# Converting the second layer's weights in three steps instead of two, and storing the experts' results one piece at a time

## The chip, the core and the metric

The kernel runs on one core of a Trainium2 chip. The time is device microseconds (us) from the start to the end of one execution. A core has five engines, each working through its own list of instructions in order: TensorE (PE; its weight loads are shown apart as PEld), VectorE (DVE), ScalarE (ACT), GpSimd (POOL), and SyncE (SP), which here does nothing but issue transfers. An instruction that waits holds up all that stand behind it on the same engine.

## The reference, cut to what matters

```python
attn = retention(q, k, v)               # state = gamma * state + k v^T ; y = scale * q state
x = attn as 1536 rows of 512
logits = x @ w_gate + softplus(x @ w_noise) * noise
top2, weights = the two best of 8 experts for each row, softmax over the two
for e in range(8):                      # D = 512, F = 1024
    h = max(x[mask] @ w1[e], 0)
    out[mask] += weight * (h @ w2[e])
h = out @ w_in                          # second layer: w_in 512x1024, w_out 1024x512
s = h * softmax(h);  ln = (s - mean) / sqrt(var + 1e-6) * g_ln
result = ln @ w_out
```

The two weights of the second layer, `w_in` and `w_out`, arrive as 64-bit floats, since the reference divides them by a square root in that type. The chip works on 32 bits, so the kernel converts them itself, with integer arithmetic.

## The kernel before

First comes the retention and the choice of experts (to about 98 us of the profiled execution), then eight experts one after the other (to about 376 us), then the second layer over twelve tiles of 128 rows.

**An expert** `e` is computed for up to `CAPS[e]` rows (448 falling to 384). Every 32-bit product is made of three matmuls: each operand is split into a high and a low part. The first half of an expert is eight blocks `hidden(e, f, ...)` (L709) of twelve matmuls each. A block ends in a PSUM bank; ACT writes the high part `hh` of the result (L722), then DVE the low part `hl` (L723). Even blocks use the two banks of tag `b`, odd blocks the two of tag `a`, so block f=4 can only start when `hl` of block f=0 is written. The second half is four calls of `second(e, j, py)` (L1051), 24 matmuls each, into four banks `c0` to `c3`.

**Weights.** An expert has eight units of 512 KB (units 8e to 8e+7). `load_unit` brings one into a tile `wr`, of which there are four; `split_unit` makes the high part `wh` on ACT (L194) and the low part `wl` on DVE (L195), and with that the `wr` is free for a later load. `advance(e, j)` (L1066) is called after every second block (j = 0 to 3) and after every `second` (j = 4 to 7): it splits units up to a bound out of the table `AHEAD` and issues loads to three units further. All loads of experts 2 to 7 are issued by SP.

**Rows.** The rows of expert e+2 are gathered by POOL while expert e is computed, stored to DRAM (`xs`, L999) and read back turned (`xq`, L1006), all by SP; `xg_t` (L1010) turns and splits the rows of the next expert behind the first and the second `second` of an expert: DVE L1023, ACT L1025, DVE L1026, four times.

**Results.** `y_t(e - 1, d)` (L1036) turns the result of the expert before into `yr` (DVE L1043, one buffer). It is called behind blocks 1, 3, 4 and 5 of expert e. The last call, behind block 5, issues four stores to `yg` from SP at once (L1047), ahead of the weight load of `advance(e, 2)`. `yg` is read back after the last expert.

**Conversion.** `convert_steps` (L93) is a generator over 16 jobs, 128 x 512 numbers each: eight of `w_in`, then eight of `w_out`. Each call of `convert()` runs it to the next `yield`. Before, a job has two steps. One step is three operations on DVE (L117, L118, L119) and one on ACT (L120), which needs the third. The other step is two operations on DVE (L123, L124), the first of which needs ACT's; then SP stores the result (L125) and loads the input of the job after the next (L102, two buffers). Six calls are made in expert 0, in `advance` of j = 4 to 7; then five in each expert, behind blocks 2 and 6 and in `advance` of j = 5, 6 and 7. Ahead of the last expert `for _ in conv` (L1129) runs what is left, which before is nothing. The second layer's weights are read back from DRAM by SP during the last expert (`w_in`, L174) and at its end (`w_out`, L176).

The order on each engine is the order of the calls in the program: nothing plans it anew.

Of the kernel before, what the change touches and what calls it, by code (L numbers as in the profile page):

```python
# [44 lines left out]
def retnet_moe_solu(ctx, tc, qT, kT, k, v, w_gate, w_noise, noise, w1, w2, w_in, w_out, g_ln,  # L45
                    decay, out, dbg=None):
    nc = tc.nc
    B, NC, _, H, D = v.shape
# [3 lines left out]
    E = w1.shape[0]  # L52
# [40 lines left out]
    def convert_steps():  # L93
        V = nc.vector
        cv = conv_ctx.enter_context(tc.tile_pool(name="cv", bufs=1, side="right", reuse_waits="tile"))
        view = lambda x, c: x.rearrange("(p r) f -> p (r f)", p=128)[:, c:c + 512]

        def load(n):
            if n < len(conv_jobs):
                w, _, c = conv_jobs[n]  # L100
                t = cv.tile([128, 512], I64, tag="raw", name="raw", bufs=2)
                nc.sync.dma_start(t, view(w, c))  # L102
                raws.append(t)

        raws = []
        load(0)
        for n, (w, f, c) in enumerate(conv_jobs):
            load(n + 1)
            yield
            raw = raws.pop(0)  # L110
            bits = raw.bitcast(I32).rearrange("p (n t) -> p n t", t=2)
            l, h = raw.bitcast(U32).rearrange("p (n t) -> p n t", t=2)[:, :, 0], bits[:, :, 1]
            m, e = (cv.tile([128, 512], I32, tag=t, name=t) for t in ("cm", "ce"))
            t = m.bitcast(F32)
            o = cv.tile([128, 512], F32, tag="co", name="co", bufs=2)

            V.tensor_scalar(m, h, 0xFFFFF, 1 << 20, op0=OP.bitwise_and, op1=OP.bitwise_or)  # L117
            V.scalar_tensor_tensor(t, l, 2.0 ** -32, m, op0=OP.mult, op1=OP.add)  # L118
            V.tensor_scalar(e, h, 0x7FF00000, None, op0=OP.bitwise_and)  # L119
            nc.scalar.activation(e, e, AF.Relu, bias=rebias, scale=8.0)  # L120
            yield

            V.scalar_tensor_tensor(e, h, -2 ** 31, e, op0=OP.bitwise_and, op1=OP.bitwise_or)  # L123
            V.scalar_tensor_tensor(o, t, 2.0 ** -20, e.bitcast(F32), op0=OP.mult, op1=OP.mult)  # L124
            nc.sync.dma_start(view(f, c), o)  # L125

    conv = convert_steps()

    def convert():
        next(conv, None)  # L130
# [74 lines left out]
    def feed(split_to, load_to, later=None):  # L205
        while feed_at[0] < min(split_to, n_units):
            while feed_at[1] <= feed_at[0]:
                load_unit(feed_at[1])
                feed_at[1] += 1
            split_unit(feed_at[0], later)  # L210
            feed_at[0] += 1
        while feed_at[1] < min(load_to, n_units):
            load_unit(feed_at[1])
            feed_at[1] += 1
# [367 lines left out]
    def add_table(lo, tag="a"):  # L582
        oh, nm = HOT.pop(lo)
        last = oh.shape[1] - 1
        p = bank(tag, (128, 32))
        for n in range(last + 1):
            nc.tensor.matmul(p, oh[:, n], nm[:, n], start=(n == 0), stop=(n == last))
        nc.vector.tensor_add(table, table, p)
# [3 lines left out]
    def by_rows():  # L592

        m = [128, 4, 32]
        nc.vector.tensor_mul(spread, part4[:, :, None].to_broadcast(m), table[:, None, :].to_broadcast(m))
# [113 lines left out]
    def hidden(e, f, c, between=None):  # L709

        xh, xl = xgT[e]
        hh, hl = H_t[e]
        early_part = not e and c.start == 0
        p = bank(("b", "c0", "b", "c1")[f % 4] if early_part else "ba"[f % 2])[:, :c.stop - c.start]

        terms = [(unit_t[8 * e + d][n], x, d) for x, ns in ((xh, (0, 1)), (xl, (0,))) for d in range(KD) for n in ns]
        for n, (w, x, d) in enumerate(terms):
            nc.tensor.matmul(p, w[:, 0, f * 128:(f + 1) * 128], x[:, d, c],  # L718
                             start=(n == 0), stop=(n == len(terms) - 1))
        if between:  # L720
            between()
        nc.scalar.activation(hh[:, f, c], p, AF.Relu)  # L722
        nc.vector.scalar_tensor_tensor(hl[:, f, c], p, 0.0, hh[:, f, c], op0=OP.max, op1=OP.subtract)  # L723
# [7 lines left out]
    def hidden_of(e):  # L731
        H_t[e] = (ep.tile([128, KF, CAP], F32R, tag="hh", name="hh"),
                  ep.tile([128, KF, CAP], F32R, tag="hl", name="hl"))
# [223 lines left out]
    xr_t, PY, yr_t = {}, {}, {}  # L957
# [78 lines left out]
    def y_t(e, d):  # L1036

        if d == 0:  # L1040
            yr_t[e] = ep.tile([128, CAP // 32, KD, 32], F32, tag="yr", name="yr")
        n = SETS[e]
        nc.vector.transpose(yr_t[e][:, :n, d], PY[e][d][:, :32 * n])  # L1043
        if d == KD - 1:
            dst = yg[OFF[e]:OFF[e + 1], :].rearrange("(b i) (a c) -> a i b c", i=32, a=4)
            for a in range(4):
                nc.sync.dma_start(dst[a], yr_t[e][32 * a:32 * a + 32, :n].rearrange("p b d j -> p b (d j)"))  # L1047
            yr_t.pop(e)
            PY.pop(e)

    def second(e, j, py):  # L1051

# [12 lines left out]

    def advance(e, j):  # L1066
        up = 8 * e + (AHEAD[j] if e or j > 3 else 5 + j)
        for n in range((0, 0, 0, 0, 2, 2, 1, 1)[j] if not e else j > 4):
            convert()
        feed(up, up + 3)  # L1070

    for e in range(E - 1):
        if e:
            hidden_of(e)
        for j in range(4):
            for f in (2 * j, 2 * j + 1):
                hidden(e, f, slice(0 if e else EARLY, CAPS[e]))
                if not e and f == 0:
                    todo = slots(10, NT)
                    next(todo)  # L1080
                if not e and f == 1:
                    next(todo, None)
                if not e and f == 3:
                    add_table(4, "c2")
                    add_table(10, "c3")
                    by_rows()
                if not e and f == 5:
                    lists()
                    for _ in load_xg(1):
                        pass  # L1090
                    rt_ctx.close()
                    gx["pool"] = gx_ctx.enter_context(tc.tile_pool(name="gx", bufs=1, side="right"))
                if e == 1 and f in (1, 3):
                    next(rows, None)
                if e and e + 2 < E and f < 4:
                    fresh = fresh if f else load_xg(e + 2)
                    nc.gpsimd.tensor_copy(pace, H_t[e][0][:1, f, :1])  # L1097
                    next(fresh)
                if e and f in (5, 7):
                    next(fresh, None)  # L1100
                if e and f in (1, 3, 4, 5):
                    d = (1, 3, 4, 5).index(f)
                    y_t(e - 1, d)
                    y_bank(e, d)
                elif e and f in (2, 6):
                    convert()
                elif not e and f > 5:
                    for d in ((0, 1), (2, 3))[f - 6]:
                        y_bank(e, d)
            advance(e, j)  # L1110
        for j in range(4):
            unit_t.pop(8 * e + j)
        xgT.pop(e)
        py = PY[e]
        for j in range(4):
            second(e, j, py)
            for d in ((0, 1), (2, 3), (), ())[j] if e else ((), (0, 1), (2, 3), ())[j]:
                xg_t(e + 1, d)
            advance(e, 4 + j)
            if not e:  # L1120
                fresh = fresh if j else load_xg(2)
                for n in range(2 if j < 2 else 1):
                    next(fresh)
                rows = fresh
            elif j in (1, 2):
                next(fresh, None)
# [4 lines left out]
    e = E - 1  # L1131
    hidden_of(e)
    for j in range(4):
        for f in (2 * j, 2 * j + 1):
            hidden(e, f, slice(0, CAPS[e]))
            if 0 < f <= KD:
                y_t(e - 1, f - 1)
            if f == 5:
                weights()
        advance(e, j)  # L1140
# [21 lines left out]
    for b in range(3):  # L1162
        py = bank(f"c{b}")
        c = slice(b * 128, (b + 1) * 128)
# [73 lines left out]
    with tc.If(full == 1), ExitStack() as fb_ctx:  # L1238
        fb = fb_ctx.enter_context(tc.tile_pool(name="fb", bufs=1))
        psum_pool(fb_ctx, "psum3", a=2, b=2, d0=1)  # L1240
        for g in range(NT // 4):
            xT = fb.tile([128, KD, 4, 128], F32, tag="fx", name="fx")
            acc, gate = [], []
            for n in range(4):
# [3 lines left out]
                p = bank("a")  # L1248
# [9 lines left out]
                a = fb.tile([128, DM], F32, tag=f"fa{n}", name="fa")  # L1258
# [10 lines left out]
            for e in range(E):  # L1269
                wa, wb = load_w(w1[e], w2[e])  # L1270
                h = fb.tile([128, KF, 512], F32, tag="fh", name="fh")
                for f in range(KF):
                    p = bank("b")
# [5 lines left out]
                for n in range(4):  # L1279
                    p = bank("a")  # L1280
# [6 lines left out]
            for n in range(4):  # L1287
                i = 4 * g + n
                x2T = fb.tile([128, DM], F32, tag="fr", name="fr")
                p = bank("a")  # L1290
# [12 lines left out]
                for f in range(KF):  # L1303
                    p = bank("a", (128, 128))
                    nc.tensor.transpose(p, z[:, f * 128:(f + 1) * 128], ident)
                    nc.vector.tensor_scalar_mul(zT[:, f], p, gcol[:, f:f + 1])
                p = bank("b")
                for f in range(KF):
                    nc.tensor.matmul(p, zT[:, f], wb[:, f], start=(f == 0), stop=(f == KF - 1))
                o = fb.tile([128, DM], F32, tag="fo", name="fo")  # L1310
# [57 lines left out]
```

## Time and profile before

| | us |
|---|---|
| three executions | 522.32, 525.71, 526.3 |
| their median | 525.71 |
| the profiled execution | 524.1 |
| its span in the trace | 522.5 |
| PE busy | 508.3 (97%) |
| DVE busy | 370.0 (71%) |
| ACT busy | 231.2 (44%) |

The span is the time between the first and the last instruction of the trace; 1.6 us of the execution lie outside it. The granted TensorE clock is 0.999 of full speed, so the engine's speed plays no part. A busy PE is not a PE at its peak: the ends of matmuls are modelled. Idle time of another engine costs something only where PE comes to wait for it.

### The profile page before, as it was taken

To read this page: it belongs to the slowest core of one execution; us is meant where nothing else is said; L and a number is where in the kernel's file an instruction comes from. 1 tells how busy PE (TensorE), PEld (TensorE's weight loads), DVE (VectorE), ACT (ScalarE), POOL (GpSimd) and SP (SyncE) were. 2 spreads that over 40 slices of the span, in tenths; PEclk is the share of its full clock that TensorE was granted. 3 is DMA by queue.
4 is the path that set the end of the run, shared out by engine and by line. 5 is a ranking of instruction groups with operands and counts; after the bars stand their busy time and mean duration, and the time that the engine had idled before them with its cause. 6 is when DMAs were issued, how large, how long until landed. Compare 5 with 4: busy or idle time off the path is not lost.

```text
span 522.5 us, 8643 instructions
## 1 busy us (share of the span) xinstructions
PE 508.3 (97%) x3068; PEld 462.9 (89%) x3068; DVE 370.0 (71%) x750; ACT 231.2 (44%) x435; POOL 102.5 (20%) x202
## 2 busy tenths in 40 slices
PE   9999999999999999999997999999999999999996
PEld 8888888999999999999997999998887788888886
DVE  5679888667668777877668778778367667766650
ACT  3487733435234335334244344354354535454441
POOL 4000001530302201204004000002244335511120
PEclk9999999999999999999999999999999999999999
DMA  8998431697897997969977987847462655563341
GB/s 252 336 398 311 167 112 52 191 346 236 263 316 178 334 319 164 336 218 221 375 241 204 325 222 213 243 143 194 150 207 58 204 166 143 169 188 102 100 122 46
DMA packets 71857, 111.92 MB, mean 214 GB/s; under 512 B 9760, under 2 KB 37152, under 8 KB 71808
## 3 DMA queue, kind: packets, MB, share of 16 engines
q1 hardware_dynamic: 65520, 94.58, 60.2%
q0 software_dynamic: 4944, 16.39, 9.8%
q8 instruction: 26, 0.43, 0.3%
q10 hardware_dynamic: 1344, 0.34, 0.3%
q14 instruction: 23, 0.19, 0.1%
HBM read 83.50 MB, written 27.79 MB: 213 GB/s over the span
## 4 chain that ended last, share of the span: by engine, by line
PE 41%; DVE 22%; DMA 17%; issue 8%; ACT 6%; SPq 4%; POOL 1%; POOLq 0%; DVEq 0%; ACTq 0%
PE b L946 12%; DMA wr<-in_moe_w_dram 9%; PE d L859 9%; DVE wl L195 4%; PE c L1060 3%; PE c L1174 3%; DVE xt L1023 3%; PE b L718 3%; DMA xq<-xs 2%; ACT wh L194 2%; PE a L718 2%; DMA xs<-xr 2%; PE s L426 2%; SPq L1047 2%; ACT xh L1025 2%
## 5 line engine op out<-in xcount | busy, mean ns | idle before, releaser
L195 DVE TENSOR_TENSOR wl<-wr,wh 128x1024 fp32r<-128x1024 f32 x68 | 81.8, 1219 | 30.6 <-ACT wh L194 26.3
L194 ACT ACTIVATE wh<-wr 128x1024 fp32r<-128x1024 f32 x68 | 70.1, 1051 | 33.6 <-DMA wr<-in_moe_w_dram 33.3
L1060 PE MATMUL c<-hh,wh 128*128 128x448 f32 (+5 forms) x224 | 79.2, 353 | 0.3 <-DVE c L1034 0.3
L1060 PE MATMUL c<-hl,wh 128*128 128x448 f32 (+5 forms) x224 | 78.8, 352 | 0.0
L1060 PE MATMUL c<-hh,wl 128*128 128x448 f32 (+5 forms) x224 | 78.7, 351 | 0.0
L718 PE MATMUL b<-xh,wh 128*128 128x192 f32 (+8 forms) x144 | 47.3, 337 | 3.6 <-DVE hl L723 3.2
L718 PE MATMUL b<-xh,wl 128*128 128x192 f32 (+8 forms) x144 | 46.8, 333 | 0.0
L1060 PEld LDWEIGHTS c<-hh,wh 128*128 128x128 f32 x224 | 42.0, 188 | 2.0 <-issue 0.6
L718 PE MATMUL a<-xh,wh 128*128 128x256 f32 (+7 forms) x128 | 43.1, 341 | 0.3 <-DVE hl L723 0.2
L1060 PEld LDWEIGHTS c<-hh,wl 128*128 128x128 f32 x224 | 42.1, 188 | 1.2
L1060 PEld LDWEIGHTS c<-hl,wh 128*128 128x128 f32 x224 | 42.1, 188 | 1.1
L718 PE MATMUL a<-xh,wl 128*128 128x256 f32 (+7 forms) x128 | 42.9, 340 | 0.0
L946 PE MATMUL b<-wh,zh 128*128 128x512 f32 (+1 forms) x104 | 38.5, 376 | 0.5 <-ACT zh L935 0.5
L859 PE MATMUL d<-wh,x2h 128*128 128x512 f32 x96 | 38.8, 404 | 0.0
L946 PE MATMUL b<-wl,zh 128*128 128x512 f32 (+1 forms) x104 | 38.4, 375 | 0.0
L859 PE MATMUL d<-wl,x2h 128*128 128x512 f32 x96 | 37.9, 395 | 0.0
L859 PE MATMUL d<-wh,x2l 128*128 128x512 f32 x96 | 37.8, 394 | 0.0
L1097 POOL COPY pace<-hh 1x1 f32<-1x1 f32 x20 | 8.7, 433 | 138.0 <-ACT hh L722 137.9
L120 ACT ACTIVATE ce<-ce,rebias 128x512 int32<-128x512 int32 x16 | 11.6, 723 | 54.1 <-DVE ce L119 51.3
L1025 ACT ACTIVATE xh<-xt 128x428 fp32r<-128x428 f32 (+5 forms) x24 | 13.0, 540 | 50.8 <-DVE xt L1023 50.8
L989 POOL DMA_INDIRECT xr<-xd,rows_r x27 | 30.1, 1116 | 14.8 <-issue 5.1
L872 ACT ACTIVATE ee<-d,st 128x1024 f32<-128x1024 f32 x12 | 13.4, 1118 | 41.8 <-DVE st L865 41.8
(259 smaller groups left out, 1096.3 us busy)
## 6 DMA issues: line engine op xcount, KB each, us to landing
wr<-in_moe_w_dram SPq DMA_DIRECT2D x60, 512.0 KB
zd<-zs SPq DMA_DIRECT2D x40, 128.0 KB
zc<-zd SPq DMA_DIRECT2D x10, 512.0 KB
xs<-xr SPq DMA_DIRECT2D x18, 256.0 KB
raw<-in_moe_w_in_dram SPq DMA_DIRECT2D x8, 512.0 KB
raw<-in_moe_w_out_dram SPq DMA_DIRECT2D x8, 512.0 KB
xq<-xs SPq DMA_DIRECT2D x16, 208.0 KB
yg<-yr SPq DMA_DIRECT2D x16, 208.0 KB
```

The costliest lines, as they stand in the source:

```text
L120: nc.scalar.activation(e, e, AF.Relu, bias=rebias, scale=8.0)
L194: nc.scalar.activation(hi, t, AF.Copy)
L195: low = lambda: nc.vector.tensor_sub(lo, t, hi)
L718: nc.tensor.matmul(p, w[:, 0, f * 128:(f + 1) * 128], x[:, d, c], start=(n == 0), stop=(n == len(terms) - 1))
L859: nc.tensor.matmul(PH[i][:, s, :], x[:, c], w[:, 0, f], start=(n == 0), stop=(n == 3 * KD - 1))
L872: nc.scalar.activation(ee, ph, AF.Exp, bias=col(0), accum_out=col(1))
L946: nc.tensor.matmul(p, z[:, f * 128:(f + 1) * 128], unit_t[8 * E + 4 + f // 2][n][:, f % 2, c], start=(m == 0), stop=(m == len(terms) - 1))
L989: nc.gpsimd.indirect_dma_start(out=t[b], out_offset=None, in_=xd[:], in_offset=bass.IndirectOffsetOnAxis(ap=rows_r[:, e - 1, b:b + 1], axi ...
L1023: nc.vector.transpose(t[:, :32 * n], xr_t[e][:, :n, d:128:KD])
L1025: nc.scalar.activation(hi, t, AF.Copy)
L1060: nc.tensor.matmul(py[d][:, :CAPS[e]], c, h[:, f, :CAPS[e]], start=(f == 0 and n == 0), stop=(f == KF - 1 and n == 2))
L1174: nc.tensor.matmul(py, h[:, f, c], w[:, f % 2], start=(f == 0 and n == 0), stop=(f == KF - 1 and n == 2))
```

## The change

Three things are changed.

A conversion job has three steps instead of two. The first step issues the store of the job before and does the three operations on DVE. The second issues the load for the next job and does ACT's operation. The third does the last two operations on DVE; their store is kept for the next job's first step. The first call of all only issues the first load.

The calls of `convert()` are spread otherwise: in expert 0 one for each `advance` of j = 4 to 7 (four), and in each expert from 1 to 6 seven: behind blocks 0, 2, 6 and 7, and in `advance` of j = 5, 6 and 7.

`y_t` becomes a generator. After the turn behind block 5 it stops; the four stores follow singly: behind `advance(e, 2)`, behind block 6, behind `advance(e, 3)`, and behind `advance(e, 4)`. For the result of expert 6, in the last expert, the four stores are issued at once as before.

```diff
         raws = []
         load(0)
+        store = None
         for n, (w, f, c) in enumerate(conv_jobs):
-            load(n + 1)
             yield
+            if store:
+                nc.sync.dma_start(*store)
             raw = raws.pop(0)
...
             V.tensor_scalar(e, h, 0x7FF00000, None, op0=OP.bitwise_and)
+            yield
+
+            load(n + 1)
             nc.scalar.activation(e, e, AF.Relu, bias=rebias, scale=8.0)
             yield
 
             V.scalar_tensor_tensor(e, h, -2 ** 31, e, op0=OP.bitwise_and, op1=OP.bitwise_or)
             V.scalar_tensor_tensor(o, t, 2.0 ** -20, e.bitcast(F32), op0=OP.mult, op1=OP.mult)
-            nc.sync.dma_start(view(f, c), o)
+            store = (view(f, c), o)
+        nc.sync.dma_start(*store)
...
+            y = yr_t.pop(e)
+            PY.pop(e)
             for a in range(4):
-                nc.sync.dma_start(dst[a], yr_t[e][32 * a:32 * a + 32, :n].rearrange("p b d j -> p b (d j)"))
-            yr_t.pop(e)
-            PY.pop(e)
+                if e < E - 2:
+                    yield
+                nc.sync.dma_start(dst[a], y[32 * a:32 * a + 32, :n].rearrange("p b d j -> p b (d j)"))
...
-        for n in range((0, 0, 0, 0, 2, 2, 1, 1)[j] if not e else j > 4):
+        if j > 4 or not e and j == 4:
             convert()
         feed(up, up + 3)
...
                     d = (1, 3, 4, 5).index(f)
-                    y_t(e - 1, d)
+                    y_st = y_t(e - 1, d)
+                    next(y_st, None)
                     y_bank(e, d)
-                elif e and f in (2, 6):
+                elif e:
                     convert()
+                    if f == 6:
+                        next(y_st, None)
...
             advance(e, j)
+            if e and j > 1:
+                next(y_st, None)
...
             advance(e, 4 + j)
+            if e and j == 0:
+                next(y_st, None)
```

## Rows read from the trace of the kernel before

**Rows 1.** The page: each engine's busy time, share of the span, instructions.
```profile
PE 508.3 (97%) x3068; PEld 462.9 (89%) x3068; DVE 370.0 (71%) x750; ACT 231.2 (44%) x435; POOL 102.5 (20%) x202
```

**Rows 2.** Waits of PE: who waited for whom, us, times, longest.
```profile
PE c L1060 <- DVE c L1034: 0.3, 1, 0.3
```

**Rows 3.** Timeline, PE, 205 to 323 us: start, length, instruction, idle before it.
```profile
206.57 0.45 PE L718 MATMUL b<-xh,wh 128*128 128x412 f32 x1 [0.56 <-DVE hl L723]
...
270.16 0.45 PE L718 MATMUL b<-xh,wh 128*128 128x396 f32 x1 [0.17 <-ACT xh L1025]
...
277.78 0.34 PE L718 MATMUL a<-xl,wh 128*128 128x396 f32 x1
280.74 0.45 PE L718 MATMUL b<-xh,wh 128*128 128x396 f32 x1 [2.62 <-DVE hl L723]
...
322.01 0.44 PE L718 MATMUL a<-xh,wh 128*128 128x388 f32 x1 [0.24 <-DVE hl L723]
```

**Rows 4.** Timeline, DVE, experts 4 to 5.
```profile
273.85 1.23 DVE L195 TENSOR_TENSOR wl<-wr,wh 128x1024 fp32r<-128x1024 f32 x1 [1.74 <-ACT wh L194]
274.99 0.68 DVE L123 SCALAR_TENSOR_TENSOR ce<-raw,ce 128x512 int32<-128x512 int32 x1
275.71 0.69 DVE L124 SCALAR_TENSOR_TENSOR co<-cm,ce 128x512 f32<-128x512 f32 x1
...
277.46 0.42 DVE L117 TENSOR_SCALAR cm<-raw 128x512 int32<-128x512 int32 x1
277.91 0.69 DVE L118 SCALAR_TENSOR_TENSOR cm<-raw,cm 128x512 f32<-128x512 uint32 x1
278.52 0.42 DVE L119 TENSOR_SCALAR ce<-raw 128x512 int32<-128x512 int32 x1
280.11 0.57 DVE L723 SCALAR_TENSOR_TENSOR hl<-b,hh 128x396 fp32r<-128x396 f32 x1 [1.18 <-ACT hh L722]
...
281.08 0.61 DVE L1043 STREAM_TRANSPOSE yr<-c 128x416 f32<-128x416 f32 x1
...
284.08 0.56 DVE L723 SCALAR_TENSOR_TENSOR hl<-b,hh 128x396 fp32r<-128x396 f32 x1
```

**Rows 5.** Timeline, ACT, the same stretch.
```profile
278.97 0.72 ACT L120 ACTIVATE ce<-ce,rebias 128x512 int32<-128x512 int32 x1 [4.20 <-DVE ce L119]
279.60 0.48 ACT L722 ACTIVATE hh<-b 128x396 fp32r<-128x396 f32 x1
```

**Rows 6.** Waits of ACT and of SP's queue, whole span.
```profile
ACT ce L120 <- DVE ce L119: 51.3, 15, 4.4
...
SPq L125 <- DVE co L124: 56.0, 13, 8.3
SPq L176 <- DVE wl L195: 37.4, 19, 8.9
```

**Rows 7.** Timeline, SP, expert 4: start, time of issue, instruction.
```profile
252.16 4.96 SPq L1047 DMA_DIRECT2D yg<-yr  x4
...
261.74 5.37 SPq L176 DMA_DIRECT2D wr<-in_moe_w_dram  x3
```

**Rows 8.** The chain that ended last, expert 4: start, us, what.
```profile
241.93 13.35 DMA wr<-in_moe_w_dram
```

**Rows 9.** Windows: length, then PE, PEld, DVE, ACT, POOL, clock, DMA share, GB/s.
```profile
249.00:256.00 7.00, 7.00 (x40) 7.00 (x39) 3.15 (x7) 1.22 (x3) 0.31 (x1) 1.00 1.03 401
...
270.00:277.00 7.00, 6.84 (x37) 6.84 (x38) 5.05 (x8) 2.73 (x4) 0.00 (x0) 1.00 0.33 75
```

**Rows 10.** Timelines of DVE and PE in the last expert.
```profile
344.58 0.56 DVE L723 SCALAR_TENSOR_TENSOR hl<-b,hh 128x384 fp32r<-128x384 f32 x1 [1.71 <-ACT hh L722]
346.60 0.56 DVE L723 SCALAR_TENSOR_TENSOR hl<-a,hh 128x384 fp32r<-128x384 f32 x1 [1.46 <-ACT hh L722]
...
354.92 0.56 DVE L723 SCALAR_TENSOR_TENSOR hl<-a,hh 128x384 fp32r<-128x384 f32 x1 [0.95 <-ACT hh L722]
...
360.74 0.33 PE L703 MATMUL a<-unit,causal 128*128 128x128 f32 x1
```

More of the change, by code (lines that the diff above doesn't have):

```diff
@@ L1136, in retnet_moe_solu @@
             if 0 < f <= KD:
-                y_t(e - 1, f - 1)
+                for _ in y_t(e - 1, f - 1):
+                    pass
             if f == 5:
```

## The prediction

> **What bounds the kernel now.** I read the page's busy times first: PE works 508.3 of 522.5 us [rows 1]. So PE sets the end, and a change that leaves its matmuls alone can only give back what PE stands idle in the stretch that the change touches. That is the second view, PE's waits, and its timeline over the experts. Five gaps are named there: 0.56, 0.17, 2.62 and 0.24 us, and 0.3 ahead of a first matmul into a result bank [rows 2, 3]. Together 3.9 us. After a gap the first matmul takes 0.45 instead of 0.34 us [rows 3], so each costs about 0.11 more. **About 4.4 us is all that the change can win among the experts**, although other engines wait far longer there: ACT 51.3 us for the third conversion operation, SP 56.0 us for the conversion's last [rows 6]. The reader should see these two sums and not take them for the prize: they are idle time of engines that are not the bound.
>
> Third, I asked the timelines of DVE and ACT what made the largest gap. In expert 5 block f=4 needs the low part of block f=0, which DVE writes at 280.11 [rows 4]. DVE was late because of three conversion steps between the experts: three operations (not shown again, the same as those at 277.46), two at 274.99, three at 277.46 [rows 4]. Twice DVE then stood idle, 1.74 us for the high part of a weight and 1.18 us for the high part of the block [rows 4], and both times that part stood on ACT behind the conversion's own operation, which had been waiting for DVE: 4.20 us before the second one, with the block's high part directly behind it [rows 5]. The two engines hold each other up in turn.
>
> **The change, part by part.**
>
> *Fewer conversion operations between two experts.* The first step is 0.42 + 0.69 + 0.42 = 1.53 us of DVE, the last 0.68 + 0.69 = 1.37 us [rows 4]. Between the `second` calls and block 0 of the next expert there were three steps out of two kinds, here 1.53 + 1.37 + 1.53 = 4.43 us. Afterwards the same three calls are, in whatever order, one of each of three kinds: 1.53 + 0 + 1.37 = 2.90 us. That is 1.53 us less.
>
> *ACT's operation a step later.* It now stands a call behind the DVE operation that it needs, and the two idle times of DVE, 1.74 + 1.18 = 2.92 us, have no cause left. In expert 5 it stands behind the high part of block 0, not ahead of it. Together with the step before, `hl` of block 0 comes 1.53 + 2.92 = 4.45 us earlier: it ends at 280.11 + 0.57 - 4.45 = 276.23 us. PE ran out of work at 280.74 - 2.62 = 278.12 us. The margin is 1.9 us, so the whole gap of 2.62 us goes. The gap at 206.57 has the same place between experts 2 and 3; the one at 322.01 comes in expert 6 behind an ACT operation of the conversion, which is no longer there at that block. I take out the three: 0.56 + 2.62 + 0.24 = 3.42, with 3 x 0.11 for the slow first matmuls **3.75 us**. The bounds are 0 (DVE late for other reasons) and 4.4 (all five).
>
> *Stores of the conversion and loads a step later.* SP no longer waits for work just given to DVE. The weight loads behind it, though, wait for `wl` as well, 37.4 us in all [rows 6], and `wl` comes out of the same list of DVE. PE waits for no weight at all. I take nothing; the bounds are 0 and the two gaps left, 0.17 + 0.3 with their slow matmuls 0.7 us. A load is issued two calls ahead of its use, as before, but calls are now seven and not five to an expert, so the notice falls by a third or so on average; at the shortest, from the last `advance` of an expert to block 2 of the next, lie three blocks. PE does 40 matmuls in 7 us [rows 9], so a block of 12 takes 2.1 us and the three 6.3 us. What covers a late load is the spare PSUM bank: about 2.1 us, worked out under the rivals.
>
> *Result stores singly.* The four took 4.96 us of SP's issue in expert 4 [rows 7], and the weight load of `advance(e, 2)` came behind them. It now comes about 5 us sooner. No wait of PE hangs on it, hence nothing. The load which was really late there, 13.35 us to land [rows 8], had been issued at 241.93, ahead of those stores.
>
> The DMA engines were fully busy around it, 1.03 by the share [rows 9], and what is moved ahead in the queue is only exchanged there for something else. The Trainium skill says as much ("DMA: Bandwidth & Descriptors", Issuing engines are not separate DMA queues): whatever engine issues them, transfers run on the same 16 DMA engines and interleave. By that rule the reordering of stores and loads gives no time; the row at 249 us agrees, the row at 270 us with its share of 0.33 shows that this does not hold for the whole stage.
>
> *What is left over for the last expert.* This speaks against the change. Sixteen jobs of three steps need 49 calls, counting the first load and the final store. There are 4 + 6 x 7 = 46. Three steps are therefore run at once ahead of expert 7: three operations on DVE, one on ACT, two on DVE, 1.53 + 0.72 + 1.37 = 3.62 us, which nothing separates [rows 4, 5]. And the last three calls of expert 6 now carry 2.90 us where before only one step of 1.37 us was left. That makes 3.62 + 2.90 - 1.37 = 5.15 us more in DVE's time ahead of 355 us. DVE's idle time there, waiting for blocks that PE had not finished, is 1.71 + 1.46 + 0.95 = 4.12 us [rows 10]. About 1.0 us is not covered and delays the small operations that build `causal`, which PE already takes up with hardly a pause at 360.74 [rows 10]. I put **+1.0 us** into the sum; bounds 0 (short idle times between DVE and ACT take it up) and 5.15 (none of the idle time serves). The blocks themselves have room: `hl` of block 0 would end at 344.58 - 1.71 + 5.15 + 0.56 = 348.6 [rows 10]; PE, done with block 0 at about 344, needs it three blocks later, at about 350.
>
> **The sum:** 524.1 - 3.75 + 1.0 = 521.35, which I give as **521.3 us** for the time of an execution. The sum starts from the profiled execution; the median of the three shown lies 1.6 us above it, at 525.71. I assume that the others differ by gaps of the same kind, so nothing is added. Against the median it is 4.4 us or 0.8% less. A difference under 1%, 5.26 us here, can't be told from no change; the limits are 520.45 and 530.97.
>
> **The rivals.**
>
> *More goes than the named gaps.* The window with a share of 0.33 shows DMA engines without work [rows 9]. If loads start earlier there, the two small gaps go too, and if DVE finds room before the last expert, the 1.0 us is not paid: 524.1 - 4.4 = 519.7. Against it: those loads waited for `wl`. Chance 0.14.
>
> *No change, since the DMA engines set DVE's pace.* DVE's lateness in expert 4 starts with the weight that took 13.35 us [rows 8]. If, with the engines full, it lands 2 us later still because other stores and loads stand ahead, the margin of 1.9 us is gone, and the 2.62 us gap stays or moves to another expert: between 524.1 and the median, 525.7. That is the rule cited above, taken as a mechanism. Chance 0.17.
>
> *Slower: the last quarter of the result is stored too late.* `yr` has one buffer. Its fourth store now stands behind the two loads of `advance(e, 4)`; in expert 4 three loads were issued from 261.74 to 267.11 [rows 7], so the store goes out at about 265.5. Block 1 of the next expert writes `yr` again, at 281.08 before [rows 4], some 4.45 us sooner afterwards: 276.6. That leaves 11.1 us for landing. `hl` of block 2 stands behind it, at 284.08 before [rows 4], hence ending at 284.08 + 0.56 - 4.45 = 280.2, and block 6 needs it two blocks after 278.12, at 282.3: 2.1 us of cover. From a landing time of 13.2 us on, each microsecond is lost at each of five such places. The longest landing above was 13.35 [rows 8]. At 16 us it would cost 5 x 2.8 = 14 us: 535. For it: a full DMA queue. Against it: one such landing was the exception. Chance 0.06.
>
> **How the numbers follow.** The forecast has 0.63; its own range is 519.7 (all five gaps, nothing paid in the last expert) to 523.4 (half of what lies between 1.0 and the bound of 5.15 paid as well, 2.1 us). About a third of it, 0.21, I place below 520.45, since the runs at 525.7 and 526.3 suggest that typical executions hold more waits than the profiled one. With the first rival that makes 0.35 for faster by over 1%. Slower by over 1% has 0.06. The rest, 0.59, is within 1%. The range reaches from 518.3, the first rival with a little for the spread of executions, to 525.6 at the no-change case.
>
> **What would show it.** Right: no gap of PE for `hl` between experts 4 and 5; ACT's wait for L119 far below 51.3 us; SP's wait for L124 nearly gone; conversion operations directly ahead of expert 7's first `hl`, and PE's transpose at L703 about 1 us later behind its matmuls. Wrong: a DVE wait at L1043 for a store, or at L117 for a load; new gaps of PE in the last expert; PE's gaps for `hl` as large as before.

## The result, and the profile after

| | before | after |
|---|---|---|
| median | 526.0 us (6 executions, 522.32 to 526.99) | 519.19 us (6 executions, 518.11 to 519.96) |
| profiled execution | 524.1 us | 519.29 us |
| its span | 522.5 us | 517.6 us |

The ratio is 0.989, with a 95% interval of 0.9859 to 0.992: about 1.1% faster. Timed once more beside the last experiments (e10), the changed kernel gave 0.9928 (0.9904 to 0.9952), so 0.7 to 1.1% is a fair size. The kernel before also varies more from execution to execution (519.4 to 527.0 over all that were run) than the changed one (518.1 to 520.3).

The page of the kernel after, engines' busy time; it answers to [rows 1]:

```profile
PE 506.3 (98%) x3068; PEld 462.9 (89%) x3068; DVE 370.1 (71%) x750; ACT 233.5 (45%) x435; POOL 98.4 (19%) x202
```

The number of instructions is the same on every engine; the span is 4.9 us shorter. To see where, one looks for PE's first matmul of each stage. Kernel before: second half of expert 0, expert 1, second layer.

```profile
98.80 0.37 PE L1060 MATMUL c<-hh,wh 128*128 128x448 f32 x1
...
120.10 0.36 PE L718 MATMUL b<-xh,wh 128*128 128x448 f32 x1
...
376.57 0.39 PE L859 MATMUL d<-wh,x2h 128*128 128x512 f32 x1
```

Kernel after, the same three places (line numbers are some 6 to 8 higher):

```profile
99.13 0.37 PE L1068 MATMUL c<-hh,wh 128*128 128x448 f32 x1
...
121.27 0.36 PE L724 MATMUL b<-xh,wh 128*128 128x448 f32 x1
...
371.75 0.39 PE L865 MATMUL d<-wh,x2h 128*128 128x512 f32 x1
```

The front end came 0.33 us later, the second half of expert 0 took 22.14 instead of 21.30 us (+0.84), experts 1 to 7 took 250.48 instead of 256.47 us (-5.99), and the second layer 145.85 instead of 145.93 us (-0.08). The sum is -4.90 us. All of the gain lies in experts 1 to 7: from first matmul to first matmul, experts 2, 3, 5 and 6 took 0.75, 0.83, 3.45 and 1.01 us less, and experts 1, 4 and 7 the same within 0.1 us.

PE's waits among the experts, kernel after; they answer to [rows 2, 3]:

```profile
PE a L1025 <- DVE xl L1032: 0.5, 1, 0.5
...
PE a L709 <- DVE causal L704: 0.2, 1, 0.2
```

None of the five gaps of before is left, not even the two that the prediction left in. There is one new gap in expert 0, of 0.55 us, which answers for most of the +0.84. (This stretch varies without any change to it: in the trace of e5, the same program up to there, it took 21.53 us.) Next DVE between experts 4 and 5; these rows answer to [rows 4]:

```profile
265.24 1.23 DVE L201 TENSOR_TENSOR wl<-wr,wh 128x1024 fp32r<-128x1024 f32 x1 [0.99 <-ACT wh L200]
266.39 0.68 DVE L128 SCALAR_TENSOR_TENSOR ce<-raw,ce 128x512 int32<-128x512 int32 x1
267.11 0.69 DVE L129 SCALAR_TENSOR_TENSOR co<-cm,ce 128x512 f32<-128x512 f32 x1
267.71 1.22 DVE L201 TENSOR_TENSOR wl<-wr,wh 128x1024 fp32r<-128x1024 f32 x1
268.85 0.42 DVE L119 TENSOR_SCALAR cm<-raw 128x512 int32<-128x512 int32 x1
269.31 0.69 DVE L120 SCALAR_TENSOR_TENSOR cm<-raw,cm 128x512 f32<-128x512 uint32 x1
269.91 0.42 DVE L121 TENSOR_SCALAR ce<-raw 128x512 int32<-128x512 int32 x1
271.32 0.57 DVE L729 SCALAR_TENSOR_TENSOR hl<-b,hh 128x396 fp32r<-128x396 f32 x1 [0.98 <-ACT hh L728]
```

DVE now stands idle ahead of `hl` because PE has only just finished the block, no longer because ACT is held up. ACT confirms it (answers to [rows 5]): its high part waits for PE, and the conversion's operation follows it.

```profile
270.78 0.50 ACT L728 ACTIVATE hh<-b 128x396 fp32r<-128x396 f32 x1 [4.62 <-PE b L724]
271.18 0.71 ACT L125 ACTIVATE ce<-ce,rebias 128x512 int32<-128x512 int32 x1
```

The 0.99 us ahead of the first `wl` are still ACT's: its conversion operation stood at 263.56, ahead of that weight's high part. The waits of ACT and SP after, against [rows 6]:

```profile
ACT ce L125 <- DVE ce L121: 11.7, 6, 4.1
ACT wh L200 <- DMA wr<-in_moe_w_dram: 8.7, 2, 7.6
...
SPq L182 <- DVE wl L201: 93.7, 26, 8.3
...
SPq L111 <- DVE co L129: 8.5, 5, 3.3
```

ACT's wait for the conversion fell from 51.3 to 11.7 us, SP's wait for its result from 56.0 to 8.5 us. SP waits more for `wl` instead, 93.7 against 37.4 us: it comes to its weight loads sooner and stands ready when a buffer is freed. And ACT's wait for weights from DRAM, not shown ahead of the prediction, is 8.7 us. Before it was:

```profile
ACT wh L194 <- DMA wr<-in_moe_w_dram: 33.3, 13, 5.8
```

Both waits left are in expert 0. From expert 1 on no weight is late. Two windows of the kernel after (columns as in [rows 9]) show DMA engines fully at work at 228 us and at 270 us, where the share in the second had been 0.33:

```profile
228.00:235.00 7.00, 7.00 (x40) 7.00 (x39) 5.60 (x8) 2.75 (x4) 0.00 (x0) 1.00 1.10 240
...
270.00:277.00 7.00, 7.00 (x41) 7.00 (x40) 4.43 (x8) 3.90 (x6) 3.52 (x5) 1.00 1.08 319
```

**One number for lateness.** How late DVE is can be read off the trace for each expert: from its first matmul to the end of its first `hl`. For expert 5 before, it is 280.11 + 0.57 - 268.75 = 11.93 us; after, 271.32 + 0.57 - 268.34 = 3.55 us. PE needs this `hl` after four blocks, that is after 9.3 us in expert 2, 8.6 us in expert 5 and 8.3 us in expert 7. One block, ACT's high part and DVE's low part alone make about 3.5 us, so 3.5 is the floor. For experts 2 to 7:

| kernel | 2 | 3 | 4 | 5 | 6 | 7 |
|---|---|---|---|---|---|---|
| before | 9.09 | 9.63 | 7.41 | 11.93 | 8.05 | 3.45 |
| after | 3.76 | 3.66 | 3.60 | 3.55 | 3.49 | 6.11 |
| e1_y_single | 8.91 | 8.53 | 7.18 | 9.59 | 8.02 | 3.44 |
| e2_conv_only | 3.78 | 3.66 | 3.60 | 3.54 | 3.49 | 6.12 |
| e3_act_early | 3.77 | 3.66 | 3.60 | 3.55 | 3.49 | 7.40 |
| e4_sp_early | 3.76 | 3.65 | 3.60 | 3.54 | 3.48 | 6.12 |
| e5_no_rest | 3.76 | 3.66 | 3.60 | 3.54 | 3.48 | 3.43 |
| e6_rest_two | 3.76 | 3.66 | 3.60 | 3.54 | 3.48 | 11.60 |
| e7_before_no_act | 5.29 | 4.66 | 3.60 | 3.54 | 3.49 | 3.43 |
| e8_before_sp_late | 5.52 | 4.67 | 4.02 | 5.60 | 5.17 | 3.43 |
| e9_spread_only | 3.76 | 3.66 | 3.60 | 3.54 | 3.49 | 7.40 |
| e10_changed | 3.76 | 3.66 | 3.61 | 3.55 | 3.49 | 6.12 |
| e11_before_sp_late | 6.57 | 5.71 | 4.36 | 5.61 | 5.16 | 3.42 |
| e12_convert_behind | 3.79 | 4.53 | 3.59 | 6.92 | 6.00 | 3.43 |

Each row is one traced execution. The traced execution of e1 is the fastest of its twelve (519.86 us), so its row is a mild case.

### The profile page after: what moved, and what is told of

Its sections match the earlier page's. It is cut to its first block, busy times and chain, and to the rows that moved or that the text cites. A ratio compares the mean times of both kernels' runs of the same rounds, so it can differ in the third digit from the quotient of the medians.

```text
span 517.6 us, 8642 instructions
## 1 busy us (share of the span) xinstructions
PE 506.3 (98%) x3068; PEld 462.9 (89%) x3068; DVE 370.1 (71%) x750; ACT 233.5 (45%) x435; POOL 98.4 (19%) x202
## 4 chain that ended last, share of the span: by engine, by line
PE 74%; DVE 13%; issue 6%; DMA 3%; ACT 2%; POOL 0%; SPq 0%; POOLq 0%; DVEq 0%; ACTq 0%
PE c L1068 18%; PE b L952 12%; PE b L724 11%; PE a L724 10%; PE d L865 10%; PE c L1190 3%; PE s L432 2%; DVE wl L201 2%; PE c L449 2%; DMA wr<-in_moe_w_dram 2%; PE c L460 1%; DVE pm L436 1%; PE c L445 1%; DVE rt L510 1%; PE c L482 1%
## 5 line engine op out<-in xcount | busy, mean ns | idle before, releaser
L728 ACT ACTIVATE hh<-b 128x192 fp32r<-128x192 f32 (+8 forms) x36 | 17.1, 476 | 43.6 <-PE b L724 40.6
L728 ACT ACTIVATE hh<-a 128x256 fp32r<-128x256 f32 (+7 forms) x32 | 15.9, 497 | 45.3 <-PE a L724 45.3
```

## The experiments

**Theory A**, the prediction's: DVE and ACT held each other up over the conversion, and there was too much of it between two experts. **Theory B**: SP's waits for the conversion held up weight loads, and late weights made DVE late.

| kernel | median, us | kernel before on the same chip, us | ratio, 95% interval |
|---|---|---|---|
| e1_y_single | 523.31 | 523.42 | 1.0004 (0.9976 to 1.0032) |
| e2_conv_only | 518.96 | 523.42 | 0.9907 (0.9872 to 0.9942) |
| e3_act_early | 520.14 | 523.42 | 0.994 (0.9915 to 0.9965) |
| e4_sp_early | 518.48 | 523.42 | 0.9907 (0.9874 to 0.9941) |
| e5_no_rest | 518.61 | 523.27 | 0.9926 (0.9899 to 0.9954) |
| e6_rest_two | 524.06 | 523.27 | 1.0011 (0.9987 to 1.0036) |
| e7_before_no_act | 518.51 | 523.27 | 0.9903 (0.9869 to 0.9937) |
| e8_before_sp_late | 518.06 | 523.27 | 0.99 (0.9867 to 0.9933) |
| e9_spread_only | 519.89 | 522.79 | 0.9955 (0.993 to 0.998) |
| e10_changed | 518.8 | 522.79 | 0.9928 (0.9904 to 0.9952) |
| e11_before_sp_late | 518.32 | 522.79 | 0.9921 (0.9893 to 0.995) |
| e12_convert_behind | 530.17 | 522.79 | 1.0147 (1.0106 to 1.0188) |

**Which part carries the gain: e1 and e2.** e1 puts only the changed `y_t` and its calls, as in the diff of the change, into the kernel before. e2 is the changed kernel with

```diff
-                if e < E - 2:
+                if e < E - 2 and a < 0:
                     yield
```

> The kernel before, with the experts' result stores singly as in the changed kernel and the conversion as it was. If DVE and ACT holding each other up over the conversion made the gaps (theory A), the gaps stay: 526.0 us, within 1 us, and ACT still waits about 50 us for the third conversion operation. If weight loads held up on SP made DVE late (theory B), the weight load that stood behind the four stores comes 5 us sooner and part of the gain is seen: 522 to 524.

> The changed kernel with the four result stores issued at once again. Theory A: all of the gain stays, 519.2 us, within 0.7. Theory B: 521 to 523, and gaps of PE for hl come back between experts.

e1 gave nothing beyond its interval of 0.3% either way, e2 all. The result stores, one half of the change's description, do not matter; it is the conversion.

**Inside the conversion: e3 and e4**, the changed kernel with ACT's operation early again, and with stores and loads early again:

```diff
 # e3
+            nc.scalar.activation(e, e, AF.Relu, bias=rebias, scale=8.0)
             yield
 
             load(n + 1)
-            nc.scalar.activation(e, e, AF.Relu, bias=rebias, scale=8.0)
             yield
 # e4
+            load(n + 1)
             yield
-            if store:
-                nc.sync.dma_start(*store)
...
-            load(n + 1)
...
-            store = (view(f, c), o)
-        nc.sync.dma_start(*store)
+            nc.sync.dma_start(view(f, c), o)
```

> The changed kernel with ACT's conversion operation back in the step of the three DVE operations; loads and stores stay a step later. Theory A: ACT's wait for DVE comes back, to about 50 us, and with it idle times of DVE of 1 to 2 us at each conversion; but between two experts only one such step is left instead of one or two, so part of the gaps comes back: 520 to 522.5. Theory B: no change from 519.2.

> The changed kernel with the conversion's stores and loads as before: the store right behind the last DVE operation, the next load right behind the store, ACT's operation still in a step of its own. Theory A: SP's wait for the last conversion operation comes back, some 40 us or more, and PE does not feel it: 519.2, within 0.7. Theory B: weight loads come late behind that wait: 521 to 524.

e4 agrees with theory A: SP waits 53.6 us for the conversion again, and the time does not feel it (518.48 us, at the lower edge of what was expected). e3 has the time that theory A gave, but not for its reason. ACT's wait is back, 46.1 us, and yet there is no gap between experts; the lateness is at its floor. What e3 loses (its median is 1.2 us above that of e2; the intervals overlap) is one wait in the last expert, for the small operations that build `causal` (1.48 us instead of 0.18); expert 7 takes 36.23 us in its trace and 34.91 in that of e2. So neither half is needed as long as the rest of the change, the new spread of the calls, stays.

**Each half alone in the kernel before: e7 and e8.** e7 takes out ACT's operation, e8 moves only stores and loads:

```diff
 # e7
-            nc.scalar.activation(e, e, AF.Relu, bias=rebias, scale=8.0)
 # e8
         load(0)
+        store = None
         for n, (w, f, c) in enumerate(conv_jobs):
-            load(n + 1)
             yield
+            if store:
+                nc.sync.dma_start(*store)
...
             nc.scalar.activation(e, e, AF.Relu, bias=rebias, scale=8.0)
+            load(n + 1)
             yield
...
-            nc.sync.dma_start(view(f, c), o)
+            store = (view(f, c), o)
+        nc.sync.dma_start(*store)
```

> The kernel before without ACT's conversion operation (the converted weights are then wrong; the DVE operations and all transfers stay). Theory A: ACT and DVE no longer hold each other up, hl of block 0 of expert 5 comes about 2.9 us sooner, and most of the gaps go: 520 to 522. Theory B: 525 to 526, since SP waits for DVE as before.

> The kernel before, two steps to a job and five calls to an expert, with only the stores and loads moved: the store in the next job's first step, the load behind ACT's operation of that step. Theory A: SP's wait for the last conversion operation falls from 56 us to under 15, and the time stays at 526, within 1. Theory B: 520 to 523.

Both give the full gain, 4.8 and 5.2 us. In this gain e7 was as theory A had it and e8 as theory B had it; their times lie below the ranges because the kernel before stood at 523.27 us this time, not at 526. e8 refutes theory A's claim that SP's part is worth nothing. e7 takes ACT's operation out; it does not move it a step later, as the change does, and that edit alone was not run. The timeline of DVE in e8, between experts 4 and 5, is the most telling of the study:

```profile
265.87 1.22 DVE L199 TENSOR_TENSOR wl<-wr,wh 128x1024 fp32r<-128x1024 f32 x1 [1.74 <-ACT wh L198]
...
272.14 0.57 DVE L727 SCALAR_TENSOR_TENSOR hl<-b,hh 128x396 fp32r<-128x396 f32 x1 [1.18 <-ACT hh L726]
```

The two idle times of [rows 4], 1.74 and 1.18 us, are there unchanged, to the hundredth, and so are the three conversion steps. But `hl` comes at 272.14 and not at 280.11, since everything ahead of it started earlier. So the three steps and the two idle times alone do not make a gap: DVE had come late to them. ACT's waits in e8 say why:

```profile
ACT ce L122 <- DVE ce L121: 49.9, 15, 4.4
ACT wh L198 <- DMA wr<-in_moe_w_dram: 6.1, 4, 3.4
```

The weights are no longer late: 6.1 us of waiting against 33.3. Note that e7, which touched no transfer, also lowered that wait, to 19.6 us. That led to **theory C**, a ring: late weights make DVE late, a late DVE frees the weight buffers late, so SP issues the next loads late, and weights come late. ACT's operation in its old place and SP's wait are two links.

The traces show the links. A unit's load needs the `wr` of the unit four before, so it can't go out ahead of the end of that unit's `wl`. One turn of the ring in the kernel before, three loads into the same buffer (the first went out at 241.93 [rows 8], the second at 261.74 [rows 7]); ACT, DVE, DVE, SP, ACT:

```profile
255.30 1.06 ACT L194 ACTIVATE wh<-wr 128x1024 fp32r<-128x1024 f32 x1 [5.78 <-DMA wr<-in_moe_w_dram]
...
256.39 1.23 DVE L195 TENSOR_TENSOR wl<-wr,wh 128x1024 fp32r<-128x1024 f32 x1 [4.11 <-ACT wh L194]
...
276.32 1.22 DVE L195 TENSOR_TENSOR wl<-wr,wh 128x1024 fp32r<-128x1024 f32 x1
...
279.87 3.54 SPq L176 DMA_DIRECT2D wr<-in_moe_w_dram  x2
...
288.84 1.06 ACT L194 ACTIVATE wh<-wr 128x1024 fp32r<-128x1024 f32 x1 [2.45 <-DMA wr<-in_moe_w_dram]
```

The late weight holds up DVE for 4.11 us and frees its buffer at 257.62; the load at 261.74 is split behind the conversion steps by 277.54; the next goes out at 279.87 and is late again. Over the loads of units 16 to 59, counted in the traces from the first matmul of the expert before, the loads of e8 go out 5.7 us earlier on average than in the kernel before. Of this, 1.7 us are SP's shorter delay once the buffer is free (1.99 instead of 3.68 us), and 4.0 us are buffers freed earlier. In e7 SP's delay is nearly what it was (3.45 us), and the loads still go out 4.4 us earlier.

**The third cut: e9, and controls.** e9 makes both edits, ACT's of e3 and SP's of e4; e10 is the changed kernel itself, e11 is e8 again.

> The changed kernel with neither of the two cures: ACT's conversion operation stands in the step of the three DVE operations, and store and load go out as before, the store right behind the last DVE operation. What is left of the change is that seven calls instead of five share the work, and the result stores singly. Theory C, formed after the first eight runs: late weights make DVE late, a late DVE frees the weight buffers late, and so weights come late; ACT's operation in its old place and SP's wait are two links of that ring, and either cut ends it. If the ring needs both links and they are back, the gaps are back: 522 to 524. If the even spread is a third cut (one conversion job between two experts instead of one and a half, 1.5 us less of DVE), 519 to 521.

> The changed kernel itself, for comparison on the same chip: 519.2, within 1.

> The kernel before with only the conversion's stores and loads a step later, once more, beside the changed kernel: 518.1, within 0.7, so about 1 us below the changed kernel, which has the leftover ahead of the last expert and a late weight in expert 0.

e9 keeps ACT's wait (46.1 us) and SP's (47.7 us), and the lateness is at the floor in experts 2 to 6. Seven short steps instead of five, and one conversion job between two experts instead of one and a half, are enough alone (the result stores singly, which e9 keeps too, gave nothing in e1). Which of the two it is, the fewer operations between experts or the even spread, was not separated. So two of the change's parts suffice each alone (e8, e9), and so does taking out what the third one moves (e7). The median of e9 is still 1.1 us above that of e10 (the intervals overlap, but 11 of e9's 12 executions lie above 519.5 us and 10 of e10's 12 do not), for a reason that is not between experts; its longest wait of PE:

```profile
PE a L705 <- DVE causal L700: 1.5, 1, 1.5
```

It is the same wait as in e3, and the lateness of expert 7 is the same, 7.40 us. Both kernels have the leftover ahead of the last expert together with ACT's operation in its old place; a run of them without the leftover was not made. e11 and e10 can't be told apart: the gain of about 1 us that I expected for e11 was 0.5 us, within the intervals.

**The leftover: e5 and e6**, with three calls more and three less.

```diff
 # e5, e6
                     y_bank(e, d)
+                    if e > 3 and f == 4:     # e5
+                        convert()
                 elif e:
-                    convert()
+                    if e < 6 or f == 7:      # e6
+                        convert()
```

> The changed kernel with three more calls of the conversion, one behind block 4 of experts 4, 5 and 6, so that nothing is left ahead of the last expert. If the leftover costs 1.0 us, as the sum of the prediction had it, 518.2; if DVE's spare time covers it, 519.2, within 0.5. The three operations and ACT's should be gone from the place ahead of the last expert.

> The changed kernel with three calls less in expert 6 (none behind blocks 0, 2 and 6), so that two whole jobs are left ahead of the last expert instead of one. hl of its block 0 ended 2.2 us ahead of PE's need; the second job adds 3.6 to 4.4 us there, so if each job costs DVE and ACT its full length, PE waits 1.4 to 2.2 us for hl: 520.6 to 521.4. If the spare time there is larger than I count: 519.2.

In e5 the leftover is gone (lateness 3.43 in expert 7). Its median lies between the two times expected and can't decide; the traces do: expert 7 takes 34.86 us in e5 and 34.93 in the changed kernel, so one job left over costs less than 0.1 us there. Two jobs cost 5.45 us against e5, more than double of what I expected. Why, DVE's row ahead of the last expert in e6 and PE's gap show:

```profile
344.76 0.43 DVE L119 TENSOR_SCALAR cm<-raw 128x512 int32<-128x512 int32 x1 [1.79 <-DMA raw<-in_moe_w_out_dram]
```

```profile
348.99 0.69 PE L724 MATMUL b<-xh,wh 128*128 128x384 f32 x1 [3.17 <-DVE hl L729]
```

The second job's input is loaded inside the leftover, so DVE had to wait 1.79 us for it, which I had not counted. The rest is the clock, below. This trace is of the slowest execution of e6 (525.99 us), and expert 7 takes 41.14 us in it, 6.28 more than in e5.

**Another order: e12.**

```diff
-        for n in range((0, 0, 0, 0, 2, 2, 1, 1)[j] if not e else j > 4):
-            convert()
         feed(up, up + 3)
+        for n in range((0, 0, 0, 0, 2, 2, 1, 1)[j] if not e else j > 4):
+            convert()
```

> The kernel before with one thing changed: in advance, the conversion's call stands behind the weights' splits and loads, not ahead of them. SP's loads no longer queue behind the conversion's store there, and DVE frees the weight buffers first; the step's contents stay, and so does ACT's wait. Theory C: that cuts the ring at the same link as the later store: 518 to 520. If the later store worked by something else: 523 to 526.

It is slower by 1.5%, through one gap in expert 0 that neither side had foreseen:

```profile
DVE cm L117 <- DMA raw<-in_moe_w_in_dram: 5.8, 1, 5.8
```

```profile
123.35 1.97 PE L1019 MATMUL a<-unit,xr 128*128 128x128 f32 x8 [8.80 <-DVE xl L1026]
```

The conversion's first loads now stood behind three weight loads, went out at 113.37, and DVE waited for them with the split of expert 1's rows behind it. After that there is no gap between experts, but a pause of 8.8 us gives DVE time to catch up in any case, which no run tells apart from a cut of the ring. So for theory C this run is inconclusive. It does show the price of a conversion load that comes late, a risk that the prediction covered with "about 2.1 us".

## Why the prediction was right, step by step

The time lies in the range, 2.1 us below the forecast. It lies below 519.7 too, where the forecast's own range ended: only the first rival, with its chance of 0.14, reached down to it. The change was 1.1% faster; I had put 0.59 on less than 1% and 0.35 on more. So the direction and the stage were foreseen, but that the time fell into the range is in part luck: the ring, of which a single cut gives the whole gain, is not in the prediction.

- **PE bounds, and only its gaps can be won.** Right. Its gaps among experts 1 to 7 are gone, and that is the gain. The bound of 4.4 us was too low: experts 1 to 7 gained 5.99 us. Measured from start to start against the usual distance, PE lost 5.7 us from expert 1 to expert 6 before and nothing after. A named gap cost about 0.27 us on top of its length (2.88 for that of 2.62), not 0.11, and two delays in expert 2, together 0.58 us, were too short to be named.
- **Fewer operations between experts.** Right, and worth more than its 1.53 us: in e9, where it comes with the even spread alone, the lateness is at the floor.
- **ACT's operation a step later.** Right in sign as far as known: without the operation (e7) the loss is gone; the move alone was not run. The working was wrong: the two idle times of DVE, 1.74 and 1.18 us, were not what made the gap, since e8 has both and no gap, and afterwards 0.99 and 0.98 us of them were still there. `hl` of expert 5 came 8.4 us earlier against PE (11.93 to 3.55), where the step gave 4.45 with the one before. The rest is the weights that are no longer late.
- **Stores and loads of the conversion a step later: nothing.** This step was wrong as I put it. Taken alone it gives the whole gain (e8). It adds nothing only where the other two are there (e4). I had argued that loads wait for `wl` as well, which comes from DVE; that is true, but it closes a ring, and I read it as a reason that nothing could be won. That DVE's lateness in expert 4 starts with the late load of 241.93 stands in the prediction only as a rival's reason for no change; why that load was late I did not ask.
- **Result stores: nothing.** Right (e1, e2).
- **The leftover ahead of the last expert: +1.0 us.** Mis-sized. The lateness of expert 7 rose by 2.66 us (3.45 to 6.11), and PE's wait for `causal` was 0.18 us. Without the leftover expert 7 takes 0.07 us less (e5). The estimate comes nearer where ACT's operation stands in its old place: there the wait is 1.48 and 1.49 us (e3, e9).
- **Expert 0** was not in the sum: it cost 0.84 us in this trace.
- **The signs.** Those for right came, but for the transpose at L703, which waited 0.18 us and not 1. Two of those for wrong came, both too small to matter: one DVE wait of 0.2 us for a conversion load, and PE's 0.18 us in the last expert.
- **The clock** was read off one trace (0.999) and left out of the sum. In many executions of the kernel before it was lower; see the last section.

So the sum was -3.75 + 1.0 = -2.75 us. Measured between the profiled executions: -4.81 us.

Of the rivals, *more goes than the named gaps* came nearest: the two small gaps went, the leftover was not paid, and the DMA engines worked where they had idled. It gave 519.7; the profiled execution took 519.29. *The DMA engines set the pace* did not happen: weights came on time with the same bytes. The Trainium skill's rule there ("DMA: Bandwidth & Descriptors", Issuing engines are not separate DMA queues) says on which engines transfers run, not what a load loses while it waits to be issued; they idled part of the time, with a share of 0.33 in one window [rows 9]. That a new order of stores and loads gives no time, as the prediction concluded from it, does not hold here: e8 changes only the order in which they are issued and gains 5.2 us. *The last quarter stored too late* did not happen: no wait of DVE at the turn into `yr` appears.

What stays open: whether the ring is the whole cause of the late weights, and how much each link adds. Each of three cuts brings the lateness under PE's need in every expert, though not to the floor in e7 and e8, and the traces show the links and loads that go out earlier; no run changes the number of `wr` buffers, which would be another cut. Open, too, is why experts 1 and 2 take 0.77 and 0.51 us longer in the traces of e2, e7 and e12 than in all others that have no gap there; no wait is named.

## What to carry to other kernels

When two engines and a load queue wait for each other in a circle, lateness can be handed on from stage to stage, and one small cut can end it, as each of three did here; three cures are then not worth three times one. Before costing a queue's wait at nothing because another wait stands beside it, follow who that other one waits for, and see whether the chain comes back. And measure the slack by one number per stage, such as the time from the first matmul to the first result written: it shows how near to the edge a kernel stands (6.11 of about 8.3 us in the last expert here) where the time does not.

## What the runs showed of the hardware that was not expected

A pause of PE can cost more than its length. In e6 (columns as in [rows 9]) the windows around the 3.17 us gap are:

```profile
336.00:345.00 9.00, 9.00 (x54) 9.00 (x53) 5.67 (x10) 1.38 (x2) 0.00 (x0) 1.00 0.58 179
345.00:349.00 4.00, 0.83 (x6) 0.51 (x4) 3.14 (x7) 2.71 (x5) 0.00 (x0) 0.91 0.00 1
349.00:355.00 6.00, 6.00 (x19) 6.00 (x20) 6.00 (x9) 2.86 (x5) 0.00 (x0) 0.50 0.89 245
355.00:360.00 5.00, 5.00 (x30) 5.00 (x29) 3.83 (x16) 2.08 (x4) 0.00 (x0) 0.99 0.84 183
```

After the gap the granted clock was 0.50 for the next 6 us, 1.2 instead of 2.4 GHz, and PE began 19 matmuls in that time where 54 in 9 us, or 36 in 6, are usual: some 17 matmuls or 2.8 us lost on top. e12's gap of 8.80 us did the same: in the trace the matmuls of 448 columns behind it start 0.37 us apart for about 3 us, not 0.20. The gap of 2.62 us before [rows 3] had no such sequel; the matmuls of 396 columns behind it start 0.18 us apart, as ever.

The granted clock was also lower in many executions of the kernel before that were not traced. Of its 72 executions beside the experiments, 39 have a mean granted clock of 0.997 or less, with a median of 523.65 us; the other 33 have 0.998 or more, with a median of 521.54 us. None of the changed kernel's 18 executions lies under 0.998. So in many executions part of what the change wins seems to be clock, which the trace at 0.999 did not show. Which gaps come ahead of the lower clock is not shown.
